# Two kinds of row stores moved from GpSimd's DMA queue to SyncE's, and a second staging buffer, in an adaLN linear-attention and GEGLU block

## The chip, the cores and the metric

One core of a Trainium2 chip runs the whole kernel. The time is device microseconds (us) of one execution, from the host's view of the device. Six runs of the kernel before gave 766.0, 765.21, 793.06, 792.11, 784.9 and 785.91 us, so the median is 785.41 us. The profiled execution is one of them.

## The reference, cut to what matters

The input `x` has 2048 rows of 1024 bfloat16 values. One conditioning row gives six modulation rows. A linear-attention branch and a GEGLU branch follow each other, each normed, scaled, shifted and added back:

```python
mod = (_silu(c) @ w_mod).reshape(c.shape[0], 6, 1, -1)          # sa, ca, ga, sb, cb, gb
h = _layernorm(x) * (1 + ca) + sa
q, k, v = heads(h @ wqkv)                                       # 32 heads of 32
pq, pk = phi(q), phi(k)                                         # elu(t) + 1 + 1e-6
kv = einsum('bhsd,bhse->bhde', pk, v);  z = pk.sum over rows
o = einsum('bhqd,bhde->bhqe', pq, kv) / (pq . z + 1e-6)
x = x + ga * (o @ wo)                                           # "x2" below
h = _layernorm(x) * (1 + cb) + sb
out = x + gb * ((_gelu(h @ w_gate) * (h @ w_up)) @ w_down)      # F = 3584
```

## The kernel before, in words

Rows are handled in tiles of 128 (`TT` = 4 tiles make a block of 512 rows, two blocks make a group of 1024). The kernel has these phases, one after the other on TensorE:

- **Keys, values, queries** (`kvq_phase`): per block, q, k and v with a seven-product form of the matrix product, and the sums `kv` and `z`.
- **Merge** (`merge_phase`): the last query products, during which `Wp` = KV times ga times W_o is made, and the first denominators are spread over partitions through DRAM (`den_sums`, `den_mul`, tensor `den`).
- **W_o phase** (`wo_phase`, L1270 and on): sixteen tiles, `wo_tile` each. A tile loads its 128 rows of `x` into one of eight buffers of `x2_ring` (L1234), makes 16 matmuls into a pair of PSUM banks (L1239; `psC` has two pairs, so tile t+2 can't begin before the add of tile t has read its pair), adds `x` on VectorE (a helper at L549 records every `tensor_tensor`), and stores the sum to the DRAM scratch `x2_scr` (L1242, tensor name `x2s`). Tiles 0 to 7 are normed at once: ScalarE or VectorE take the statistics, VectorE writes the normed rows (L1180, `xh2_ring`, three buffers), and a DMA stores them to the DRAM scratch `xh_scr` (L1181, tensor name `xhs`). After the fourth tile of a block, `h2_load` (L1165) reads these 512 rows back with a DMA transpose on SyncE's queue, so that the GEGLU branch has them with the model dimension on partitions. ScalarE and VectorE scale and shift the transposed halves in place (L1217, L1219).
- **Gate and up of group 0** (`gate_up`, matmuls L1359 and, for the nested products, L1370): fourteen units, gate and up in turn, in the seven-product form. Beside it run three things for later: `late_norm` norms the rows of group 1 (reads `x2s` at L1191, writes `xhs` at L1203), `wd_sums` makes first-level sums of W_down on VectorE, and GpSimd's queue makes other sums of W_down by DRAM-to-DRAM DMAs, some of them accumulating (L1032, tensors `ts` and `us`), each batch released by a small GpSimd copy (L1049).
- **Down of group 0**, then gate, up and down of group 1 (L1566 and L1610).

`wd_sums(c)` runs for seven pieces c. It loads two pieces (L1083, L1084), adds them in two steps on VectorE into a buffer of `wds_ring`, and stores the two halves to `ts` from GpSimd's queue (L1090). `wds_ring` has one buffer, so the first add of piece c+1 has to wait until both stores of piece c have landed.

All of this is recorded first and then put in order by a planner (`Plan`). TensorE keeps the order of the text. For the other engines and for the DMA queues the planner simulates the program forwards and backwards with rough costs, gives every operation a due time, and issues each queue in the order it found best. So moving a DMA to another queue gives it another place among that queue's work, and shifts the order on VectorE and ScalarE too. Every engine and queue executes its own list strictly in order. DMAs of a queue take eight completion semaphores in rotation (called lanes below): a DMA waits until the one eight places earlier on its queue has landed. SyncE's queue carries all loads and both transposes; GpSimd's carries the stores of rows, the W_down moves and a few tiny operations.

Of the kernel before, what the change touches and what calls it, by code (L numbers as in the profile page):

```python
# [12 lines left out]
F16 = mybir.dt.float16  # L13
# [272 lines left out]
def kernel(  # L286
# [14 lines left out]
    P = 128  # L301
# [13 lines left out]
    NW = min(TG, D)  # L315
# [68 lines left out]
    def at(off, shape, dt):  # L384
        return Ring(off, shape, dt, 1)()
# [89 lines left out]
    def quarters(n, shape, dt):  # L475
# [20 lines left out]
    xio_ring.slots += Ring(203, [TT, NW], BF16, 1).slots  # L496
    wdr_ring = Ring(189, [2, D], BF16, 1)
    wds_ring = Ring(193, [2, 2, NW], F16, 1)
    wdt_ring = Ring(197, [2, NW], F16, 1)
    sub_a = [at(76 + 3.5 * j, [NPR // 2, HB], F16) for j in range(3)]  # L500
    sub_b = [at(189 + 3.5 * j, [NPR // 2, HB], F16) for j in range(4)]
# [19 lines left out]
    xh_scr = [[scr_pool.tile([TG, D], F16, name=f"xhs{g}_{h}", tag=f"xhs{g}_{h}") for h in range(2)]  # L521
              for g in range(NGR)]
    xa_scr = [scr_pool.tile([TG, D], F16, name=f"xas{b}", tag=f"xas{b}") for b in range(NG)]
    den_scr = [scr_pool.tile([2, P // DH, 2, KH * TG], BF16, name=f"den{pr}", tag=f"den{pr}") for pr in range(2)]
    x2_scr = [scr_pool.tile([TG, D], BF16, name=f"x2s{b}", tag=f"x2s{b}") for b in range(NG)]
# [9 lines left out]
    te, ve, ac, gp, sy = (plan.on(e) for e in ("PE", "DVE", "ACT", "POOL", "SP"))  # L535
# [12 lines left out]
    def tt_op(out, a, b, op):  # L548
        ve.tensor_tensor(out=out, in0=a, in1=b, op=op)  # L549
# [613 lines left out]
    def h2_load(g, h):  # L1163
        plan.extra = 4000
        sy.dma_start_transpose(out=hr2[:, :, h * TG:(h + 1) * TG], in_=xh_scr[g][h][:])  # L1165
        plan.extra = 0
        h2_loads[g, h] = plan.ops[-1]
# [9 lines left out]
    def ln2_xhat(tt, x2, mv, rstd, op0=ALU.subtract):  # L1177
        g, h, tl = tt // (2 * TT), tt // TT % 2, tt % TT
        xh = xh2_ring()
        ve.tensor_scalar(out=xh, in0=x2, scalar1=mv[:, 0:1], scalar2=rstd[:, 0:1], op0=op0, op1=ALU.mult)  # L1180
        gp.dma_start(out=xh_scr[g][h][tl * P:(tl + 1) * P, :], in_=xh)  # L1181
        if tl == TT - 1:
            h2_load(g, h)

# [45 lines left out]
    def wo_tile(tt, banks):  # L1230
        b, tl = tt // TT, tt % TT
        xt = x2_ring()
        plan.ahead = 24000
        sy.dma_start(out=xt, in_=x_in[tt * P:(tt + 1) * P, :])  # L1234
        plan.ahead = 14000
        psw = banks.pair()
        for half in range(NHD):
            for g in range(KD):
                te.matmul(psw[:, half, :], lhsT=pqT[b][:, g, tl * P:(tl + 1) * P],  # L1239
                          rhs=Wp[:, g, half * NW:(half + 1) * NW], start=(g == 0), stop=(g == KD - 1))  # L1240
        tt_op(xt, psw.rearrange("p h n -> p (h n)"), xt, ALU.add)
        gp.dma_start(out=x2_scr[b][tl * P:(tl + 1) * P, :], in_=xt)  # L1242
        return xt

    def merge_phase(stages):
# [33 lines left out]
    def wo_phase(ms2):  # L1279
        plan.transpose = (6000, 1000000)  # L1280
        fill = [None] * NTT
        fill[9] = h2_mods[0][0]
        fill[11] = h2_mods[0][1]
        fill[12] = h2_steps
        for tt in range(NTT):
            if tt == 4:
                for _ in range(KD):
                    ms2.step()
            if tt == 2:
                den_sums(1, psX())  # L1290
            if tt == 6:
                ms2.columns()
                ve.tensor_scalar_add(out=opcB, in0=modT[:, 4 * KD:5 * KD], scalar1=1.0)
            if tt in (3, 6):
                den_mul(den_todo.pop(0))
            xt = wo_tile(tt, psX if tt == 0 else psC)
            for h in range(2):
                if tt == AIM[h]:
                    plan.aim(h2_loads[0, h])
            if tt == NTT - 2:  # L1300
                ms2.spread(2, gbrow, 1.0)
            if tt < 2 * TT:
                if tt % 4 == 3:
                    ln2_xhat(tt, xt, *ln2_stats(xt, act_rstd))
                else:
                    ln2_xhat(tt, xt, *act_stats(xt), ALU.add)
            for f in fill[tt] or []:
                f()
# [489 lines left out]
```

## Time and profile before

| what | value |
|---|---|
| median of six runs | 785.41 us (765.21 to 793.06) |
| the profiled execution | 766.0 us, of which its span is 764.2 us; mean granted TensorE clock 0.991 |
| TensorE busy with matmuls | 732.5 us, 96% of the span |
| VectorE, ScalarE, GpSimd busy | 584.7, 431.5, 126.7 us |
| DMA traffic | 154.62 MB, 202 GB/s on average |
| W_o tiles on TensorE | from 185.1 to 258.6 us of the span |
| gate and up of group 0 | from 258.6 to about 434 us |

The span runs from the first to the last instruction; 1.8 us of the profiled execution lie outside it. The profiled execution is among the shortest of the six, 2.5% under their median. A matmul's busy time is modelled, so TensorE's share says where it stood still more than how well it worked. In the waits, each row names the waiting instruction, the instruction or DMA that came last, and then the total, the number and the longest of these waits. In the timelines, a row has its start and length in us, and in brackets the idle time of the engine just ahead of it with what ended it; SPq and POOLq rows are issues of DMAs, and a long SPq row is an issue that held SyncE's queue so long. Line numbers are those of the kernel before; the changed kernel has one line more from L499 on.

### The profile page before, as it was taken

The numbers are of one execution on the slowest core, as the hardware profiler recorded it, in microseconds if no ns is written. First come the engines' busy times: TensorE is split into PE (matmuls) and PEld (weight loads), VectorE is DVE, ScalarE is ACT, GpSimd is POOL, SyncE is SP. The second block draws the span as 40 slices with busy tenths as digits, with TensorE's granted clock in tenths as the row PEclk, the third lists the DMA queues.
The fourth block names the chain that finished last, engine by engine and source line by source line (L and its number), as shares of the span: only waits on it lengthen the run. The fifth ranks groups of instructions, "written<-read, shape, count | busy, mean of one in ns | idle before, by whom it ended". The sixth has DMA issues, their size and how long they took to land.

```text
span 764.2 us, 11450 instructions
## 1 busy us (share of the span) xinstructions
PE 732.5 (96%) x4164; PEld 389.4 (51%) x4164; DVE 584.7 (77%) x1230; ACT 431.5 (56%) x757; POOL 126.7 (17%) x206
## 2 busy tenths in 40 slices
PE   5999999999994999799999999999999999999997
PEld 2454545444441454345455476745555555558664
DVE  6899986587682876569896679757888888987763
ACT  3674676669643588588766426107777777741000
POOL 1340351000220155455340001010000000000000
PEclk9999999999997999999999999999999999999999
DMA  9847185819799799999984999853313323299822
GB/s 310 310 126 244 43 167 96 331 37 334 222 302 222 252 267 273 357 269 303 282 197 84 255 267 279 318 163 114 110 56 111 95 72 111 97 255 300 277 111 74
DMA packets 156297, 154.62 MB, mean 202 GB/s; under 512 B 34001, under 2 KB 135889, under 8 KB 154961
## 3 DMA queue, kind: packets, MB, share of 16 engines
q1 hardware_dynamic: 124944, 110.64, 48.8%
q0 software_dynamic: 28944, 41.16, 21.7%
q10 hardware_dynamic: 2352, 2.10, 0.8%
q8 instruction: 32, 0.52, 0.3%
q14 instruction: 25, 0.20, 0.1%
HBM read 127.01 MB, written 37.88 MB: 216 GB/s over the span
## 4 chain that ended last, share of the span: by engine, by line
PE 72%; DMA 11%; issue 7%; DVE 6%; POOL 2%; SPq 1%; ACT 1%; POOLq 0%; DVEq 0%
PE psum L1359 26%; PE psum L1566 13%; PE psum L1610 8%; PE psum L853 8%; PE psum L1370 6%; PE psum L923 5%; DVE mem L549 5%; PE psum L952 4%; DMA us<-in_B_w_down_dram 3%; DMA mem<-den 3%; DMA ts<-mem 2%; DMA mem<-in_A_wqkv_dram 2%; DMA mem<-in_w_mod_dram 1%; PE psum L967 1%; POOL x2s L1242 1%
## 5 line engine op out<-in xcount | busy, mean ns | idle before, releaser
L549 DVE TENSOR_TENSOR mem<-mem 128x512 f16<-128x512 f16 (+11 forms) x641 | 302.5, 515 | 44.2 <-ACT mem L1217 13.6
L1359 PE MATMUL psum<-mem 128*128 128x512 f16 x1248 | 299.5, 380 | 6.0 <-ACT mem L798 5.4
L798 ACT ACTIVATE mem<-psum 128x256 f32<-128x256 f32 (+3 forms) x284 | 154.2, 563 | 116.2 <-PE psum L1610 42.0
L549 DVE TENSOR_TENSOR mem<-psum,mem 128x512 f16<-128x512 f32 (+4 forms) x204 | 154.8, 765 | 69.8 <-ACT mem L798 25.7
L1359 PEld LDWEIGHTS <-mem 128*128 128x128 f16 (+1 forms) x1248 | 122.2, 98 | 117.5 <-issue 7.8
L1566 PE MATMUL psum<-mem 128*128 128x512 f16 (+2 forms) x462 | 99.2, 373 | 0.5 <-DVE mem L549 0.5
L1370 PE MATMUL psum<-mem 128*128 128x256 f16 x560 | 90.0, 273 | 0.5 <-ACT psum L1376 0.2
L1370 PEld LDWEIGHTS <-mem 128*128 128x128 f16 (+1 forms) x560 | 54.9, 98 | 45.6 <-issue 3.3
L1566 PEld LDWEIGHTS <-mem 128*128 128x128 f16 x462 | 45.2, 98 | 49.8 <-issue 0.7
L1239 PE MATMUL psum<-mem 128*128 128x512 f16 x256 | 58.1, 386 | 11.7 <-DVE mem L549 11.7
L1610 PE MATMUL psum<-mem 128*128 128x256 f16 (+1 forms) x588 | 66.2, 273 | 0.0
L853 PE MATMUL psum<-mem 128*128 128x512 f16 (+1 forms) x280 | 62.5, 379 | 0.0
L1610 PEld LDWEIGHTS <-mem 128*128 128x128 f16 x588 | 57.5, 98 | 9.2
L1414 ACT ACTIVATE psum<-psum 128x512 f32<-128x512 f32 x56 | 32.8, 586 | 45.2 <-PE psum L1359 28.4
L923 PE MATMUL psum<-mem 128*128 128x512 f16 x224 | 51.2, 379 | 0.0
L549 DVE TENSOR_TENSOR psum<-psum,mem 128x256 f32<-128x256 f32 x80 | 34.3, 429 | 17.4 <-ACT mem L798 15.4
L1239 PEld LDWEIGHTS <-mem 128*128 128x128 bf16 x256 | 24.8, 99 | 44.1 <-issue 14.3
L853 PEld LDWEIGHTS <-mem 128*128 128x128 f16 x280 | 27.1, 98 | 31.1
L1431 ACT ACTIVATE mem<-psum 128x512 f16<-128x512 f32 x56 | 33.3, 596 | 8.5 <-PE psum L1359 8.3
L1441 ACT ACTIVATE mem<-mem 128x512 f16<-128x512 f16 x56 | 34.5, 626 | 1.7 <-DVE mem L549 1.3
L923 PEld LDWEIGHTS <-mem 128*128 128x128 f16 (+1 forms) x224 | 21.6, 98 | 26.9 <-issue 2.0
L1217 ACT ACTIVATE mem<-mem 128x512 f16<-128x512 f16 x28 | 20.1, 804 | 19.6 <-DMA mem<-xhs 19.6
(135 smaller groups left out, 573.3 us busy)
## 6 DMA issues: line engine op xcount, KB each, us to landing
mem<-in_B_w_gate_dram SPq DMA_DIRECT2D x14, 1024.0 KB, 7.3
mem<-in_B_w_up_dram SPq DMA_DIRECT2D x14, 1024.0 KB, 12.2
mem<-in_w_mod_dram SPq DMA_DIRECT2D x24, 512.0 KB, 5.6
mem<-us SPq DMA_DIRECT2D x24, 448.0 KB, 8.4
mem<-in_A_x_dram SPq DMA_DIRECT2D x32, 256.0 KB, 6.8
ts<-in_B_w_down_dram POOLq DMA_DIRECT2D x28, 256.0 KB, 6.2
us<-in_B_w_down_dram POOLq DMA_DIRECT2D x12, 448.0 KB, 13.6
mem<-in_B_w_down_dram SPq DMA_DIRECT2D x12, 448.0 KB, 7.3
```

The lines of the kernel that those rows point to most:

```text
L549: ve.tensor_tensor(out=out, in0=a, in1=b, op=op)
L798: ac.activation(out=t, in_=ps, func=AF.Copy)
L853: te.matmul(ps, lhsT=A[:, k, i * P:(i + 1) * P], rhs=B[:, k, :], start=(start and k == 0), stop=(k == KH - 1), skip_group_check=True)
L923: te.matmul(o, lhsT=W[:, k, (j0 + i) * P:(j0 + i + 1) * P], rhs=h_form(a, k), start=(start and k == 0), stop=(k == KH - 1), skip_group_che ...
L1239: te.matmul(psw[:, half, :], lhsT=pqT[b][:, g, tl * P:(tl + 1) * P], rhs=Wp[:, g, half * NW:(half + 1) * NW], start=(g == 0), stop=(g == K ...
L1359: te.matmul(ps, lhsT=a[:, k, e, :], rhs=b[:, k, :], start=(start and k == 0), stop=(k == KH - 1), skip_group_check=True)
L1370: te.matmul(ps, lhsT=self.x[a][:, k, :], rhs=self.y[y][:, k, :], start=(start and k == 0), stop=(k == KH // 2 - 1), skip_group_check=True)
L1414: ac.activation(out=z, in_=x, func=AF.Copy)
L1431: ac.activation(out=o, in_=ps, func=AF.Gelu_apprx_tanh)
L1441: ac.activation(out=o, in_=o, func=AF.Gelu_apprx_tanh)
L1566: te.matmul(psm[:, q, c], lhsT=A[:, i, q * P:(q + 1) * P], rhs=wt[:, i, c], start=(start and i == 0), stop=(i == NPR - 1), skip_group_chec ...
L1610: te.matmul(ps[:, q, :], lhsT=a[:, k, q * P:(q + 1) * P], rhs=y[:, k, :], start=(start and q == 0 and k == 0), stop=(k == NPR // 2 - 1), s ...
```

## The change

The two stores of the W_o phase, of the sums `x2` and of the normed rows, are issued on SyncE's queue instead of GpSimd's: sixteen and eight DMAs of 256 KB. `wds_ring` gets a second buffer of 4 KB per partition at 183 KB, so that piece c+1 of `wd_sums` writes to another buffer than piece c. Nothing else in the text changes; the planner orders the whole program anew.

```diff
     wds_ring = Ring(193, [2, 2, NW], F16, 1)
+    wds_ring.slots += Ring(183, [2, 2, NW], F16, 1).slots
     wdt_ring = Ring(197, [2, NW], F16, 1)
...
         ve.tensor_scalar(out=xh, in0=x2, scalar1=mv[:, 0:1], scalar2=rstd[:, 0:1], op0=op0, op1=ALU.mult)
-        gp.dma_start(out=xh_scr[g][h][tl * P:(tl + 1) * P, :], in_=xh)
+        sy.dma_start(out=xh_scr[g][h][tl * P:(tl + 1) * P, :], in_=xh)
         if tl == TT - 1:
             h2_load(g, h)
...
         tt_op(xt, psw.rearrange("p h n -> p (h n)"), xt, ALU.add)
-        gp.dma_start(out=x2_scr[b][tl * P:(tl + 1) * P, :], in_=xt)
+        sy.dma_start(out=x2_scr[b][tl * P:(tl + 1) * P, :], in_=xt)
         return xt
```

## The prediction

> **What bounds the kernel now.** I read the page's busy shares first, then the slices, then the waits, then the timelines around the two waits that matter. In the page, TensorE is the bound nearly everywhere, and the slices show where it is not:
>
> ```profile
> PE 732.5 (96%) x4164; PEld 389.4 (51%) x4164; DVE 584.7 (77%) x1230; ACT 431.5 (56%) x757; POOL 126.7 (17%) x206
> ...
> PE   5999999999994999799999999999999999999997
> PEld 2454545444441454345455476745555555558664
> DVE  6899986587682876569896679757888888987763
> ...
> PEclk9999999999997999999999999999999999999999
> ```
>
> Slice 13 (229 to 248 us) has TensorE at 4 tenths and its clock at 7; slice 17 is the other dip. From 325 us to the end TensorE has no gap over half a microsecond, so only what happens before can move the end. The waits name both stops:
>
> ```profile
> ACT mem L1217 <- DMA mem<-xhs: 19.6, 1, 19.6
> ...
> DVE mem L549 <- ACT mem L1217: 13.6, 2, 12.6
> ...
> PE psum L1239 <- DVE mem L549: 11.7, 2, 11.3
> ...
> DVE mem L549 <- DMA ts<-mem: 8.5, 4, 5.4
> ...
> PE psum L1359 <- ACT mem L798: 5.4, 1, 5.4
> ```
>
> The first three are one chain: ScalarE waits for the transposed rows, VectorE's next instruction waits for ScalarE, and the add of W_o tile 11 stands behind it in VectorE's list, so tile 13 finds no PSUM pair. The last two are the second chain: an add of `wd_sums` waits until the stores of the piece before have landed, and a gate/up combination stands behind it. TensorE's and SyncE's timelines:
>
> ```profile
> 217.75 17.35 PE L1239 MATMUL psum<-mem 128*128 128x512 f16 x78 [0.41 <-DVE mem L549]
> 246.38 8.49 PE L1239 MATMUL psum<-mem 128*128 128x512 f16 x32 [11.28 <-DVE mem L549]
> ...
> 321.57 1.87 PE L1359 MATMUL psum<-mem 128*128 128x512 f16 x4 [5.39 <-ACT mem L798]
> ```
> ```profile
> 218.39 13.16 SPq L1165 DMA_TRANSPOSE mem<-xhs  x1
> 231.65 1.52 SPq L1234 DMA_DIRECT2D mem<-in_A_x_dram  x3
> ...
> 239.45 8.61 SPq L1165 DMA_TRANSPOSE mem<-xhs  x1
> ```
>
> The stops cost more than their length. The 32 matmuls after the first took 8.49 us, where the same number took 7.08 earlier in the phase: 1.4 us. After the second, rows of 4, 4 and 8 matmuls took 1.87, 1.06 and 2.04 us instead of 1.03, 0.60 and 1.89: 1.45 us. The stretch 239 to 249.3 us has a granted clock of 0.50. Both stops together: 11.28 + 1.41 + 5.39 + 1.45 = 19.5 us, the most that this change can win (0.9 us of small gaps apart).
>
> **What the Trainium skill says.** "TensorE: Matmul & The Clock Gate", section "What's actually happening": an idle window of about 3.4 us puts the array at half clock. The trace agrees (0.50 after 3.9 us of idleness). "DMA: Bandwidth & Descriptors", section "Issuing engines are not separate DMA queues": all issuers share 16 DMA engines. The trace agrees: the engines are 0.99 busy from 185 to 235 us, so moving stores doesn't create bandwidth, it changes who goes first. Same page, "SWDGE vs HWDGE vs iDMA": inside a DMA engine the software and hardware queues are served in turn. The trace agrees: a 256 KB store issued on GpSimd's queue at 223.44 us, after the first transpose was issued, landed only 15.9 us later, whereas the same kind of store took 5.4 us at 202.4.
>
> **The change, part by part.**
>
> *Row stores off GpSimd.* 24 issues of 0.54 us leave GpSimd. It was idle 75.1 us in front of the 16 `x2s` stores, waiting for their adds; what follows them (W_down moves) ends by 406 us and is first read at 422, so this gains nothing by itself.
>
> *Row stores on SyncE.* 24 issues of 0.4 to 0.6 us (loads take 0.37 at the median; its small `den` stores 0.6), 10 to 14 us of queue time between 191 and 260, where SyncE's issues are sparse but for the transposes. They lie beside TensorE. What counts is order. I read the instruction order of the changed program with its semaphores, and put landings to it from the trace's semaphore updates, which show that DMAs of SyncE's queue land in order: the three loads issued at 231.65 landed at 242.2, 242.9 and 243.7, right behind the transpose (241.8), the next 1 MB weight at 246.7, the second transpose at 251.1. That prices 256 KB at 0.7 us alone (1.0 for the spread `den` rows), 1 MB of weights at 3.0 and a transpose at 4.4 us once its turn has come.
>
> Now the list. The first transpose stands behind the store of tile 4's normed rows (VectorE wrote them at 213.2) and by its lane behind a `den` load eight places earlier (about 214): issued at 215 instead of 218.4. Ahead of it the queue still has stores and loads to about 220. Before, a weight of 1 MB and the load of tile 11 stood ahead of it until 227.4, and six 256 KB stores of GpSimd's queue took turns with it until 241.7. Both are now behind it. So it lands at 220 + 4.4 plus something for its start, 225 to 228, not 241.8. Behind it come three more stores of normed rows (landed by 232), the loads of tiles 11 and 12, and a weight. The second transpose waits for the last of these stores and is issued at 231 to 232 (before: 239.45, held by the store that took 15.9 us); with the weight and a store ahead it lands at 241 to 243 (before 251.1). The loads of tiles 13 and 14 now stand behind it: 242 to 244.5.
>
> TensorE: tile 11's add is now ahead of the waiting instruction in VectorE's list and needs its load, 230, so tile 13 runs without a stop from 235.1 to 238.6, tile 14 to 242.1. Tile 15 needs tile 13's add, which needs its load: 242.7 in the middle, plus 1.22 for the add, 244.0; plus 3.5 for the tile, 247.5. The tile ended at 258.6 before. Gain 11.1 us. What is late next is the load of tile 13 (a stop of about 2 us, which need not halve the clock); the scaled second half is ready at the same time, since ScalarE does the gate spread (L586) at 243 and then four short L1217.
>
> *Second staging buffer.* Piece c of `wd_sums` waits for the stores of piece c-2. The stores that ended the 5.4 us wait had been issued at 300.54 and landed 18.4 us later; the pair before had been issued at 287.50 and 288.14 and landed by 301, twelve microseconds before the stuck add. So the wait goes: 5.39 + 1.45 = 6.8 us. What is late next there is the load of the piece, landed by 310, also in time.
>
> *New.* The first pieces of `wd_sums` are loaded into space of the row buffers, so these loads stand behind stores of tiles 8 to 11 and the load of tile 15; I get 259 us for their landing where the add, moved up by 11 us, would want 257. The trace of before doesn't show this wait. Bounds: 0 (VectorE was idle a quarter of this phase) and 5 us (all of a late queue on TensorE). I take 1.
>
> Sum: 766.0 - 11.1 - 6.8 + 1.0 = 749.1 for an execution like the profiled one. I take the same 16.9 us off the median: 785.4 - 16.9 = 768.5. (The slower runs may hold longer stops; I don't know.)
>
> **The rivals.** *Only the buffer works.* If the first transpose again needs 23.4 us from its issue (its own cost, not the company's), it lands at 238.4, the second's stores at 241, the second 11.7 later at 252.4, tile 13's load at 253.5, tile 15 ends at 258.2: no gain there. Total 785.4 - 6.8 = 778.6. For it: 13.16 and 8.61 us of issue. Against: earlier transposes (L770) were issued in 4.0 us and landed in 7.5. *Only the queue works*: another wait takes the place of the buffer's, such as W_down loads late by the same 5 us. 785.4 - 11.1 = 774.3. For it: 1.09 DMA share there. Against: the landings above. *Slower:* eight lanes are too few for 24 more DMAs. If landings stay at 12 us (as GpSimd's stores), eight lanes give 0.67 DMAs per us; 18 DMAs from 201.4 us then put the first transpose's issue at 228.4, with 23.4 its landing at 251.8, three stores behind it (4.5) and the second transpose at 268, tile 13's load 269, tile 15's end 273.8: 15.2 us late, less 6.8: 785.4 + 8.4 = 793.8. It decides from a mean landing of some 10 us on; SyncE's own DMAs in 204 to 212 us took 6 to 10. That the change doesn't do what it says is excluded by the instruction order: all 24 stores stand on SyncE's list, and `wd_sums` waits for stores two pieces back.
>
> **How the numbers follow.** Likeliest (768.5, own range 765 to 773): 0.63. Only the buffer: 0.15. Only the queue: 0.14. Slower: 0.08. The fastest end is all stops gone, 785.4 - 19.5 - 0.9 = 765; runs of one kernel differ by more than a microsecond, so 763. The upper end takes in the only-buffer case with 3 us of new waits: 782. That leaves the slower case out. The limit of 2%, about what a measurement of this kernel can tell from no change, is 769.7, inside the likeliest case: two thirds of it and a little of the others are faster, 0.44; within 2% 0.50; slower by over 2% needs 801, 0.06.
>
> **What would show it.** Right: the wait of ScalarE's L1217 under 8 us; TensorE's stop in the W_o tiles under 4 us, in front of tile 15 instead of 13; gate/up starting at 246 to 249; no granted clock of 0.5 between 239 and 249; no 5.4 us stop in gate/up. Wrong: the first transpose landing after 232; a wait of VectorE for `x` rows or W_down loads that reaches TensorE; SyncE held for lanes ahead of the first transpose.

## The result, and the profile after

The changed kernel took 763.6 us in the median of 31 runs (759.9 to 797.6); 68 runs of the kernel before, spread over the same chip time, gave 770.0. The ratio of the two is 0.9942, with a 95% interval of 0.9924 to 0.9959: a gain of 0.6%, where the prediction's own sum says 2.2%. In most kernels here some executions take 10 to 40 us longer, and in each of the three such that were profiled a transpose of the down phase is held for over 30 us (the last experiment shows such a hold); the ratios leave the long executions out, and two variants had too few others for a ratio. The profiled execution took 761.16 us, its span 759.4, against 766.0 and 764.2 before. TensorE by phases, in us:

| | W_o begins | W_o | gate/up, group 0 | all after it |
|---|---|---|---|---|
| before | 185.08 | 73.50 | 175.12 | 330.5 |
| after | 186.16 | 59.72 | 182.61 | 330.9 |

So 13.8 us were won in the W_o phase, 7.5 were lost again in gate/up, and 1.1 came before both. Busy shares and slices of the changed kernel's page:

```profile
PE 733.9 (97%) x4164; PEld 389.9 (51%) x4164; DVE 585.9 (77%) x1230; ACT 432.8 (57%) x757; POOL 116.1 (15%) x182
...
PE   4999999999999878999999999999999999999997
...
PEclk9999999999999999999999999999999999999999
```

The hole in slice 13 (4 tenths, clock 7) is gone; what is left is spread over slices 14 to 16. The waits of the changed kernel (lines are one higher than before):

```profile
PE psum L1360 <- ACT mem L799: 6.4, 3, 3.4
...
DVE mem L550 <- DMA mem<-in_B_w_gate_dram: 5.6, 1, 5.6
...
ACT mem L799 <- DMA x2s<-mem: 4.6, 1, 4.6
...
ACT mem L1218 <- DMA mem<-xhs: 4.2, 1, 4.2
...
ACT mem L1196 <- DMA mem<-x2s: 2.6, 1, 2.6
...
DVE mem L550 <- DMA ts<-mem: 0.3, 1, 0.3
```

ScalarE's wait for transposed rows fell from 19.6 to 4.2 us, VectorE's for the stores of W_down sums from 8.5 to 0.3. Two of the others are new and name the moved stores: `x2s<-mem` is a store that a ScalarE copy waits for, `mem<-x2s` a load behind such stores. TensorE's timeline, with its idle time in brackets:

```profile
210.91 31.24 PE L1240 MATMUL psum<-mem 128*128 128x512 f16 x144
...
245.88 8.80 PE L1360 MATMUL psum<-mem 128*128 128x512 f16 x40
...
257.44 1.39 PE L1360 MATMUL psum<-mem 128*128 128x512 f16 x4 [2.33 <-ACT mem L799]
```
```profile
273.26 1.02 PE L1360 MATMUL psum<-mem 128*128 128x512 f16 x4 [3.39 <-ACT mem L799]
...
291.87 1.68 PE L1360 MATMUL psum<-mem 128*128 128x512 f16 x4 [2.27 <-DVE mem L550]
```

The W_o tiles run without a stop of more than 0.6 us, and in place of one stop of 5.4 us at 316 there are three at 255, 270 and 290. SyncE's timeline:

```profile
216.57 6.24 SPq L1166 DMA_TRANSPOSE mem<-xhs  x1
...
228.79 7.25 SPq L1166 DMA_TRANSPOSE mem<-xhs  x1
...
248.56 0.33 SPq L1235 DMA_DIRECT2D mem<-in_A_x_dram  x1
...
261.42 0.38 SPq L1321 DMA_DIRECT2D mem<-in_B_w_up_dram  x1
261.91 0.66 SPq L1243 DMA_DIRECT2D x2s<-mem  x1
```

The transposes hold the queue 6.2 and 7.3 us instead of 13.2 and 8.6, and by the trace's semaphore updates they landed at 225.7 and 238.1 instead of 241.8 and 251.1. The last three rows are one chain. The load at 248.56 is tile 14's; it shares a buffer with tile 6, whose store landed at 248.5. It landed at 255.1, so tile 14's sum was ready only then. Its store stood behind the second up weight, which waited for TensorE until 261.4. It landed at 271.6. The first copies of the up units go into `c1_ring`, which shares 180 to 182 KB with tile 14's buffer: ScalarE waits, and TensorE for ScalarE.

### The profile page after: what moved, and what is told of

Same layout as the page of the kernel before. It is cut to its first block, busy times and chain, and to the rows that moved or that the text cites. A ratio compares the mean times of both kernels' runs of the same rounds, so it can differ in the third digit from the quotient of the medians.

```text
span 759.4 us, 11426 instructions
## 1 busy us (share of the span) xinstructions
PE 733.9 (97%) x4164; PEld 389.9 (51%) x4164; DVE 585.9 (77%) x1230; ACT 432.8 (57%) x757; POOL 116.1 (15%) x182
## 4 chain that ended last, share of the span: by engine, by line
PE 84%; DMA 8%; ACT 4%; DVE 3%; issue 1%; SPq 1%; DVEq 0%; ACTq 0%
PE psum L1360 29%; PE psum L1567 13%; PE psum L1611 8%; PE psum L854 8%; PE psum L1371 7%; PE psum L924 5%; PE psum L1240 5%; PE psum L953 4%; DMA x2s<-mem 3%; DVE mem L550 2%; PE psum L677 2%; DMA mem<-in_B_w_gate_dram 2%; DMA mem<-in_B_w_up_dram 1%; DMA mem<-in_w_mod_dram 1%; PE psum L968 1%
## 5 line engine op out<-in xcount | busy, mean ns | idle before, releaser
L550 DVE TENSOR_TENSOR mem<-mem 128x1024 f16<-128x1024 bf16 (+11 forms) x641 | 302.9, 515 | 39.7 <-ACT mem L799 14.8
L799 ACT ACTIVATE mem<-psum 128x512 f16<-128x512 f32 (+3 forms) x284 | 154.2, 562 | 120.7 <-PE psum L1611 42.6
L1442 ACT ACTIVATE mem<-mem 128x512 f16<-128x512 f16 x56 | 34.8, 625 | 2.3 <-DVE mem L550 2.1
L1033 POOL DMA_DIRECT2D ts<-in_B_w_down_dram x28 | 29.3, 1247 | 7.7 <-DMA us<-in_B_w_down_dram 4.2
```

The source lines that it names most:

```text
L799: ac.activation(out=t, in_=ps, func=AF.Copy)
L1442: ac.activation(out=o, in_=o, func=AF.Gelu_apprx_tanh)
```

## The experiments

Two theories at first. A: each part does what was forecast, and SyncE's in-order list gives part of it back. B: the planner orders the whole program anew with every edit, and this order, not the queue, makes the differences. Later ones, Q and W, are named where they come up. Phase times are of the profiled executions; where the long hold of the last experiment is absent, all have 80.4 us for down of group 0 and 246.4 to 246.9 for group 1.

### One part alone

The second buffer alone:

```diff
+    wds_ring.slots += Ring(183, [2, 2, NW], F16, 1).slots
```

> Only the second buffer of wds_ring; the row stores stay on GpSimd's queue. Theory A (each part works where it stands, and what the stores' queue gains in the W_o phase is given back by SyncE's list in gate/up): the W_o phase keeps its 73.5 us with the stop of 11 us, gate/up of group 0 falls from 175.1 to about 168.5, ratio to before 0.991. Theory B (what costs in gate/up is the planner's new order of VectorE and ScalarE, which any edit brings): the 5.4 us stop goes, but other stops of several us appear in gate/up, ratio 0.996 to 1.004.

Ratio 0.995 (0.9921 to 0.9979), profiled 760.01 us. The 5.4 us stop is gone and a 2.5 us stop stands at 320. W_o took 69.3 us, not 73.5, though nothing in the edit touches it, and gate/up 173.1, not 168.5. Each theory has a half of this.

The stores on SyncE alone:

```diff
-        gp.dma_start(out=xh_scr[g][h][tl * P:(tl + 1) * P, :], in_=xh)
+        sy.dma_start(out=xh_scr[g][h][tl * P:(tl + 1) * P, :], in_=xh)
...
-        gp.dma_start(out=x2_scr[b][tl * P:(tl + 1) * P, :], in_=xt)
+        sy.dma_start(out=x2_scr[b][tl * P:(tl + 1) * P, :], in_=xt)
```

> Only the stores on SyncE's queue; wds_ring has one buffer. Theory A: W_o phase 59 to 61 us, gate/up of group 0 at 182 us or more (the three new stops stay, and a wait for the stores of W_down sums comes on top by 0 to 5 us), ratio 0.994 to 1.002. Theory B: W_o phase 59 to 61 us, gate/up anywhere between 170 and 185.

Profiled 755.04 us: W_o 63.6 (both theories had 59 to 61), gate/up 172.9, no stop for the staging buffer though it has only one. A fell: in this one profile the stores alone do better than both parts together.

The stores of tiles 8 to 15 back on GpSimd's queue:

```diff
-        sy.dma_start(out=x2_scr[b][tl * P:(tl + 1) * P, :], in_=xt)
+        (sy if tt < 2 * TT else gp).dma_start(out=x2_scr[b][tl * P:(tl + 1) * P, :], in_=xt)
```

> As the changed kernel, but the x2 stores of tiles 8 to 15 go back to GpSimd's queue (tiles 0 to 7 and all normed rows stay on SyncE's). Theory A: the first late-norm load no longer stands behind stores, and the store of tile 15 not behind a weight load, so the stops of 2.3 us at 255 and of 3.4 + 0.7 us at 270 go; W_o phase still 59 to 62 us, gate/up 173 to 177, ratio 0.983 to 0.987. Theory B: gate/up stays at 180 to 185, ratio 0.993 to 0.996.

Ratio 0.9901 (0.9869 to 0.9932), profiled 761.32 us. Gate/up fell to 172.5 as A had it, but W_o rose to 69.3: the second transpose, with three of these stores issued on GpSimd's queue while it was held, was held 12.1 us, and TensorE stood 7.6 us for a row load behind it.

The eighth row buffer moved:

```diff
-    x2_ring.slots += Ring(176, [D], BF16, 4).slots
+    x2_ring.slots += Ring(176, [D], BF16, 3).slots + Ring(185, [D], BF16, 1).slots
```

> As the changed kernel, but the eighth buffer of x2_ring lies at 185 KB instead of 182, where the copies of the up units (c1_ring) don't touch it. Theory A: only the stop of 3.4 + 0.7 us at 270, in which ScalarE waits for tile 15's store, goes; gate/up 177 to 179, ratio 0.987 to 0.990. Theory B: another wait takes its place, ratio 0.993 to 0.996.

No ratio. Gate/up took 175.7 us without the stop at 270, but not for the reason given: the late store is tile 14's, whose buffer is the seventh, and this edit moves tile 15's. In this plan the store happened to stand ahead of the weight.

These four can't separate queue and order, since every edit changes both. The next ones fix the planner's order first and move single entries after it: in their edits `on(engine, line)` gives an engine's entries from one line in planned order, `ahead(a, some)` and `behind(a, some)` keep those of them that stand ahead of `a` or behind it, and `put(ops, a, b)` moves `a` directly behind `b`.

### Queue and order apart

The changed kernel's order, with its stores issued on GpSimd's queue:

```diff
-                self.calls[op.line](getattr(self.engines[op.eng], op.fn), op.args, op.kw)
+                self.calls[op.line](getattr(self.engines[op.to], op.fn), op.args, op.kw)
...
         sy.dma_start(out=x2_scr[b][tl * P:(tl + 1) * P, :], in_=xt)
+        plan.ops[-1].to = "POOL"          # op.to is op.eng elsewhere; the same after the normed rows' store
```

> The planned order of the changed kernel on every other engine, with the 24 stores issued on GpSimd's queue again, at the same places of the program. If the queue is what makes the W_o phase short, the two transposes are held 12 to 14 us again, W_o goes back to 69 to 74 us, ratio 0.997 to 1.006 where the second staging buffer keeps its stop away. If the planner's order that came with the change makes it short, W_o stays at 60 to 63 us and the first transpose is issued within 8 us.

Ratio **0.9826** (0.9787 to 0.9865), 752.17 us in the median: with the kernel of the last experiment, from which the intervals don't tell it apart, the fastest of this study. W_o took 60.3 us, as in the changed kernel, without any store on SyncE's queue. Its TensorE, SyncE and GpSimd timelines (lines are two or three higher than before):

```profile
209.78 31.24 PE L1242 MATMUL psum<-mem 128*128 128x512 f16 x144 [0.43 <-DVE mem L551]
```
```profile
216.53 4.51 SPq L1167 DMA_TRANSPOSE mem<-xhs  x1
...
229.36 5.51 SPq L1167 DMA_TRANSPOSE mem<-xhs  x1
```
```profile
235.68 2.66 POOL L1245 DMA_DIRECT2D x2s<-mem  x5 [11.13 <-DVE mem L551]
```

In this order five row stores wait behind an add until 235.7 us, by when the second transpose is nearly through; one row store is issued during the first's hold, none during the second's. And gate/up took 173.9 us where the same order with the stores on SyncE took 182.6.

So what holds a transpose? Theory Q is the prediction's: stores that GpSimd's queue has beside it. Theory W: the 1 MB weight that SyncE's own queue has in flight ahead of it. The reverse swap, the order of the buffer-only variant with the stores issued on SyncE, tells them apart:

```diff
         gp.dma_start(out=x2_scr[b][tl * P:(tl + 1) * P, :], in_=xt)
+        plan.ops[-1].to = "SP"            # the same after the normed rows' store
```

> The planned order of the variant with the second staging buffer alone (its W_o took 69.3 us), where the first gate weight stands six places ahead of the first transpose, with the 24 stores issued on SyncE at the same places of the program. Theory W: with the weight still ahead the first transpose is issued in 10 us or more, W_o stays at 67 to 73, ratio 0.993 to 1.004. Theory Q: without stores on GpSimd's queue the hold falls to 5 to 8 us, W_o to 60 to 64, ratio 0.982 to 0.990.

Ratio 0.9854 (0.9800 to 0.9908). W_o fell from 69.3 to 62.1 us, with the weight still ahead of the first transpose; the numbers of theory Q hold here, not those of W. SyncE's timeline:

```profile
219.34 7.57 SPq L1167 DMA_TRANSPOSE mem<-xhs  x1
...
235.27 9.38 SPq L1167 DMA_TRANSPOSE mem<-xhs  x1
```

Theory W was tried on the kernel before itself, by moving two entries of SyncE's list and nothing else:

```diff
-            for op in self.order():
+            for op in moved(self.order()):
...
+def moved(ops):
...
+    gate, up = on("SP", 1320)[:2]
+    first, second = on("SP", 1165)[:2]
+    put(ops, up, second)                  # up weight directly behind the second transpose
+    put(ops, gate, behind(first, on("SP", 1234))[1])
+    return ops
```

> The kernel before, its order kept on every engine, stores on GpSimd's queue, one staging buffer; only two entries of SyncE's list are moved: the first gate weight (1 MB) from two places ahead of the first transpose to behind it and two row loads, and the first up weight from ahead of the second transpose to directly behind it. Theory W (a transpose is held while a large DMA issued ahead of it on its own queue is still in flight): the first transpose is issued in 4 to 8 us instead of 13.2 and landed by 226 to 230 instead of 241.8, W_o falls from 73.5 to 60 to 66, the later stop for the staging buffer (5.4 us) stays, the profiled execution is 754 to 760, ratio 0.984 to 0.992. Theory Q (stores of GpSimd's queue take turns with the transpose, as the prediction on record has it): the hold stays at 11 us or more, W_o at 70 or more, ratio above 0.996.

Ratio 1.0006 (0.9953 to 1.0060). SyncE's and TensorE's timelines:

```profile
218.00 9.67 SPq L1165 DMA_TRANSPOSE mem<-xhs  x1
...
239.47 7.17 SPq L1165 DMA_TRANSPOSE mem<-xhs  x1
```
```profile
247.46 12.73 PE L1239 MATMUL psum<-mem 128*128 128x512 f16 x48 [15.19 <-DVE mem L549]
```

The hold fell by 3.5 us, so the weight had a part in it; but the transpose landed at 238.7 us, 3.1 earlier than before and 8.7 later than the latest that theory W had. (W_o itself, 78.5 us, says nothing on the transpose: VectorE now waits 16.5 us for the moved weight, ahead of an add that TensorE needs.) Theory W falls as the main cause. What the runs have in common is the company. Row stores issued on GpSimd's queue while SyncE was held with the transpose:

| kernel, transpose | stores beside it | held, us | landed after, us |
|---|---|---|---|
| changed; first, second | 0; 0 | 6.2; 7.3 | 9.1; 9.3 |
| new order, stores on GpSimd; second | 0 | 5.5 | 7.6 |
| old order, stores on SyncE; first, second | 0; 0 | 7.6; 9.4 | 10.6; 11.4 |
| stores alone on SyncE; first, second | 0; 0 | 5.0; 7.9 | 7.0; 11.9 |
| weights moved; second | 0 | 7.2 | 9.2 |
| late stores on GpSimd; first | 0 | 6.2 | 9.0 |
| new order, stores on GpSimd; first | 1 | 4.5 | 8.4 |
| before; second | 2, at its end | 8.6 | 11.7 |
| buffer only; second | 2, at its end | 10.1 | 14.1 |
| late stores on GpSimd; second | 3 | 12.1 | 18.8 |
| weights moved; first | 6 | 9.7 | 20.7 |
| buffer only; first | 6 | 13.0 | 21.8 |
| before; first | 6 | 13.2 | 23.4 |

With no store beside it a transpose of this phase lands in 7.0 to 12.1 us, those of the variants below included; with six in 20.7 to 23.4, whatever weight stands ahead. The count alone doesn't say which causes which, since a longer hold leaves room for more stores. The pair that differs in the queue alone does: with the same order the first transpose landed after 21.8 us with the stores on GpSimd's queue, after 10.6 with them on SyncE's. Nor is it only that there was more to move: from 216 to 238 us the DMA engines were equally busy in these two profiles (a share of 1.13, counted by packets, which overlap), but moved 270 GB/s in the first and 328 in the second. For the transpose it makes no difference whether the stores leave GpSimd's queue or are only issued at another time. The Trainium skill, "DMA: Bandwidth & Descriptors", section "Queues, rings and completion order", says that each DMA engine serves its queues in turn, a whole packet at a time. That fits the direction of this table; it gives no price for a transpose, and no run here looked at single packets.

### The stops in gate/up, one at a time

Tile 14's store ahead of the second up weight (the expectations call it the third):

```diff
+    store = on("SP", 1243)[-1]
+    put(ops, ahead(store, on("SP", 1321))[-1], store)
```

> The changed kernel with its planned order kept on every engine but for one swap on SyncE's list: the last attention row to be stored (tile 14's, by its place in the program; it shares its 180 to 182 KB with two buffers of the ring that the first copies of the up unit go into) stands ahead of the third up-weight load instead of behind it. Theory A (in-order list): in the changed kernel this store was issued at 261.9 because the load ahead of it waited for TensorE until 261.4, landed at 271.6, and ScalarE's copy waited 4.6 us for it; issued at about 256 it lands at 262 to 264, the stop of 3.39 + 0.67 us at 269.9 goes, gate/up of group 0 falls from 182.6 to 178 to 179, the profiled execution from 761.2 to about 757, the ratio to the kernel before from 0.994 to about 0.989. Theory B (the order that the planner gave VectorE and ScalarE costs, and the store only happens to be last): another wait stands at the same place, gate/up stays above 181.5, ratio 0.992 or more.

Ratio 0.9904 (0.9855 to 0.9954). SyncE's and TensorE's timelines:

```profile
257.07 0.32 SPq L1243 DMA_DIRECT2D x2s<-mem  x1
257.49 0.74 SPq L1321 DMA_DIRECT2D mem<-in_B_w_up_dram  x1
```
```profile
254.64 1.02 PE L1360 MATMUL psum<-mem 128*128 128x512 f16 x4 [0.94 <-ACT mem L799]
...
266.10 1.02 PE L1360 MATMUL psum<-mem 128*128 128x512 f16 x4 [0.71 <-ACT mem L799]
```

The store landed at 264.5 us, the stop shrank from 3.4 to 0.7, and gate/up took 178.3 us, 4.3 less than in the changed kernel, as A had it. Not all of this is that stop. The first stop lies ahead of the moved entries and yet was 0.9 us instead of 2.3, so executions differ there. The third is gone as well: the gate weight, now issued at 270.6 instead of 277.7, took 5.4 us instead of 12.6. And a new stop of 2.7 us stands at 333. The ratio's interval reaches over that of the changed kernel (0.9924 to 0.9959).

Tile 8's statistics behind two copies on ScalarE:

```diff
+    stats = on("ACT", 1196)[0]
+    put(ops, stats, behind(stats, on("ACT", 799))[1])
```

> The changed kernel with one swap on ScalarE: the first statistics of the late norm (tile 8's) stand behind the two copies that TensorE waits for at 255.1, instead of ahead of them. Theory A (a late landing ahead of an urgent copy on an in-order engine): the stop of 2.33 us at 255.1 and the half clock after it (258.0 to 261.4, worth at most 1.7 us) go, gate/up of group 0 falls from 182.6 to 179 to 180.5, the profiled execution to 758 to 759, ratio about 0.990 to 0.992. Theory B: the copies wait for something else, the stop stays within 0.5 us, ratio 0.993 to 0.996.

Ratio 0.9975 (0.9946 to 1.0003). TensorE's timeline:

```profile
270.22 1.86 PE L1360 MATMUL psum<-mem 128*128 128x512 f16 x4 [5.32 <-ACT mem L799]
...
293.62 1.86 PE L1360 MATMUL psum<-mem 128*128 128x512 f16 x4 [5.11 <-DVE mem L550]
```

The first stop was 0.7 us (0.9 in the profile above, without this swap), the next two grew from 3.4 and 2.3 to 5.3 and 5.1, and gate/up took 183.8 us. TensorE only came earlier to a store and a weight; these landed at 268.6 and 292.1 us (271.6 and 290.3 in the changed kernel, where gate/up began 1.7 us later).

All three at once, the third by three W_down moves issued later on GpSimd's queue:

```diff
+    third = on("POOL", 1200)[2]
+    moves = ahead(third, on("POOL", 1033))[-3:]
+    for op in reversed(moves):
+        put(ops, op, third)
```

> The changed kernel with three swaps on in-order lists and nothing else: tile 14's store ahead of the third up-weight load on SyncE, tile 8's statistics behind two copies on ScalarE, and three weight moves on GpSimd's queue behind the next power of the late norm, about 7 us later, so that the gate-weight load issued at 277.7 has the DMA engines to itself. If the three waits are what the new queue costs and are separate, the stops of 2.33, 4.06 and 2.27 us go: gate/up of group 0 falls from 182.6 to 173 to 175, W_o stays at 59 to 61, the profiled execution is 751 to 753 and the ratio about 0.983. If a stop only moves on to the next wait (an engine that is already late), less than half of the 8.7 us comes back and the ratio stays above 0.989.

Ratio 0.9931 (0.9909 to 0.9952), gate/up 183.4 us. None of the three stops is over 0.7 us, and a new one stands at 308. TensorE's timeline, and the waits between 300 and 316 us:

```profile
313.31 1.86 PE L1360 MATMUL psum<-mem 128*128 128x512 f16 x4 [5.47 <-DVE mem L550]
```
```profile
DVE mem L1202 <- POOL mem L1200: 9.6, 1, 9.6
```

The next power of the late norm stood behind the delayed moves on GpSimd (it started at 311.8; with the first swap alone at 304.8), and VectorE waited for it. The third stop had gone with the first swap; the third swap only brought a new one.

### The stores alone again, and the long hold

The variant with the stores alone, timed anew:

> The 24 stores on SyncE with one staging buffer, as the variant of the stores alone, timed for an interval. Its profile had W_o at 63.6 and gate/up of group 0 at 172.9 us, 755.0 in all: ratio 0.982 to 0.990 if that is its ordinary time, so that the second buffer adds nothing once the order has changed; above 0.992 if that profile was a lucky one.

Ratio 1.0084 (1.0008 to 1.0160), and it can't be used: W_o (61.0) and gate/up (173.6) are as short as in its first profile, but a stop of 18.6 us stands in the down phase. All engines at that place:

```profile
438.67 30.77 SPq L1165 DMA_TRANSPOSE mem<-xhs  x1
439.13 0.60 POOL L1562 DMA_DIRECT2D mem<-ts  x1 [51.82 <-PE psum L1610]
...
469.35 5.30 PE L1566 MATMUL psum<-mem 128*128 128x512 f16 x14 [18.56 <-DMA mem<-ts]
```

The second transpose of group 1 has a 1.8 MB load of a W_down sum beside it on GpSimd's queue. The same place in the kernel before:

```profile
452.38 0.60 POOL L1562 DMA_DIRECT2D mem<-ts  x1 [51.12 <-PE psum L1610]
452.56 9.87 SPq L1165 DMA_TRANSPOSE mem<-xhs  x1
```

In the nine profiles with the short hold (9.8 to 10.9 us) the load was issued at most 0.1 us behind the transpose, mostly ahead of it; in the four with the long one (30.5 to 37.6 us) 0.3 to 0.6 us behind it. So the load was put on SyncE's queue, ahead of the transpose, in the variant with the stores alone:

```diff
+    second, load = on("SP", 1165)[3], on("POOL", 1562)[0]
+    load.to = "SP"
+    if ops.index(second) < ops.index(load):
+        put(ops, second, load)
```

> The 24 stores on SyncE with one staging buffer, and one DMA more taken off GpSimd's queue: the 1.8 MB load of a W_down sum in the first down projection (group 0), which there runs beside the second transpose of group 1, is issued on SyncE, ahead of that transpose. Theory Q again, at a second place (a transpose is slowed by what GpSimd's queue has in flight beside it): where that load was issued 0.3 to 0.6 us behind the transpose the transpose was held 30.5 to 37.6 us and TensorE stopped for 18.6 to 25.9 us at about 450 us; with the load ahead of it on the same queue the hold is 8 to 13 us, there is no stop of more than 3 us between 430 and 480 us, W_o takes 60 to 64 us, gate/up of group 0 172 to 174, the profiled execution 752 to 757 and the ratio 0.980 to 0.988. Rival (the long hold is the transpose's own, or the load's place doesn't matter): a hold of 30 us and a stop of 18 us or more there stay, the profiled execution is 770 or more. Rival (the load is needed sooner than SyncE's list can bring it): a stop of 4 to 8 us at 455 to 465 in its place, 757 to 762 in all, ratio 0.988 to 0.996.

Ratio **0.9845** (0.9804 to 0.9885), 752.98 us in the median, and all six runs lie between 750.8 and 756.9. W_o 62.0, gate/up 174.5, no stop at 450. The edit changes queue and order at once; which of them does it is not separated. SyncE's timeline:

```profile
440.99 0.35 SPq L1562 DMA_DIRECT2D mem<-ts  x1
442.08 9.24 SPq L1165 DMA_TRANSPOSE mem<-xhs  x1
```

So the stores on SyncE with one staging buffer, this one load apart, are worth what their first profile had shown (755.0 us); the second buffer isn't needed for it.

## Why the prediction was right and wrong

**The transposes.** Right in the cause: landings of 225 to 228 and 241 to 243 were forecast, 225.7 and 238.1 measured. That the stores of GpSimd's queue hold the transpose is shown by the old order with the stores on SyncE; that they do so by taking turns, as the prediction has it, no run shows. The rival in which a transpose needs 23.4 us by its own cost is out. What the prediction didn't see is that the queue isn't needed for it: the new order alone, with the stores where they were, gives W_o 60.3 us.

**W_o.** 11.1 us were forecast, 13.8 measured. Gate/up began at 245.9, just ahead of the forecast 246 to 249, because no tile stopped; the 2 us stop ahead of tile 15 was priced from a second transpose 3 to 5 us later than it came. The step took the two row loads behind that transpose for those of tiles 13 and 14; by the recorded order they are 13 and 15. Tile 14's came at 255.1 us, and its lateness went into the next phase.

**The second buffer.** Its stop is gone, as forecast (8.5 us of waits to 0.3). But its 6.8 us aren't its alone: with the stores on SyncE and one buffer there is no such stop either.

**New waits.** This is the step that failed, "Bounds: 0 [...] and 5 us [...]. I take 1." Gate/up of group 0 became 7.5 us longer although 6.8 us of stop left it, so new waits cost 14.3. Of these, idle time is 10.4 (11.1 us in all after, 0.7 before without the buffer's stop), and slower matmuls after stops the rest: after the stops of 2.33 and 2.27 us the granted clock was 0.5 for 3.4 us each (from 258.0 and 292.1 us), where the prediction had it that a stop of about 2 us need not halve the clock; after the one of 3.39 us it stayed at 1. The term was priced for one wait, that of the first `wd_sums` pieces for their space. The stops came from three others: a load of the late norm behind six stores on SyncE, tile 14's store behind a weight that waits for TensorE, and a gate weight beside W_down moves. The prediction named eight lanes as a rival for the place ahead of the first transpose only; it didn't walk SyncE's list on to 262 us and ask, for each moved store, who needs its buffer next.

**The sum.** Predicted 766.0 - 16.9 = 749.1 for the profiled execution; measured 761.2: the start 1.1 later, W_o -13.8, gate/up +7.5, the rest +0.4. That the median of 763.6 lies near the forecast 768.5 is luck: the forecast was counted from a median of six runs, 785.4, of which four were long ones, and 68 runs have 770.0.

**What the runs say of the change.** Of its two halves, the order and the queue:

| | stores on GpSimd: W_o, gate/up, ratio | stores on SyncE: W_o, gate/up, ratio |
|---|---|---|
| order of the buffer-only variant | 69.3, 173.1, 0.995 | 62.1, 177.5, 0.985 |
| order of the changed kernel | 60.3, 173.9, 0.983 | 59.7, 182.6, 0.994 |

The phase times are of one profile each. The queue wins some 7 us in W_o where the order leaves stores beside the transposes, and costs 4 to 9 us in gate/up in both. In the order that came with the change 0.6 us are left to win, and the cost remains. Why the planner found this order is not shown; it prices a DMA issue on SyncE at 450 ns and on GpSimd at 1000, and counts lanes for SyncE only.

## What to carry to other kernels

Before a DMA is moved to an in-order queue, walk that queue's new list past the place you want to help, and for every moved entry ask which buffer it frees, who writes there next, and what waits ahead of it. Where a planner orders the program, take its order and change the queue only, and the other way round: two such runs say more than undoing halves of the edit. And a stop that is removed ahead of a late DMA can be worth nothing by itself: with the first of the three nearly gone the other two only grew. Last, look at a stop in more than one profile before an edit is credited with it; here one shrank from 2.3 to 0.9 us without being touched.

## What the runs showed of the hardware

- Row stores on GpSimd's queue beside a transpose of 1 MB put off its landing: 7.0 to 12.1 us after its issue without any in the W_o phase, 18.8 with three of 256 KB, 20.7 to 23.4 with six. It is more than their bytes: with equally busy DMA engines 270 GB/s were moved with them on GpSimd's queue, 328 with them on SyncE's.
- At the second place the long and the short hold differ by a few tenths of a microsecond in the order of two issues: 9.8 to 10.9 us of hold where the 1.8 MB load on the other queue was issued ahead of the transpose or within 0.1 us, 30.5 to 37.6 us where it came 0.3 to 0.6 us behind. In the long case shown the load suffers too (439.1 to 469.3 us), and until the transpose landed the DMA engines moved 130 GB/s, against 302 in the short case of the kernel before. Why this is so wasn't tried; on one queue, with the load ahead, it didn't occur in six runs.
- A 1 MB load in flight ahead on the same queue cost the transpose's issue 3.5 us (13.2 against 9.7), and its landing 2.7, in the one pair of profiles that differs in it with the stores on GpSimd's queue.
- A stop of 2.3 us of TensorE was twice followed by 3.4 us at half the granted clock, and one of 3.4 us was not.
